# Attention, ReLU² layer and a routed second layer on one core: scatters and stores without order among themselves, another order of second-product quarters, and a later routing step

## The chip, the cores and the metric

One core of a Trainium2 chip runs the whole program. The metric is the device time of one execution in microseconds (us). The engines are TensorE (PE, with its weight loads as PEld), VectorE (DVE), ScalarE (ACT), GpSimd (POOL) and SyncE (SP); DMAs are issued from SP, ACT and POOL. In the listings, POOL issues the indirect DMAs.

## The reference

Three layers follow each other on 4608 tokens of 512 numbers.

```python
scores = scale * np.matmul(q_c, k_c.transpose(0, 1, 2, 4, 3))   # 8 x 8 heads, chunks of 64 rows
attn = softmax(scores); out = np.matmul(attn, v_c)              # becomes x: 4608 x 512
...
h = np.maximum(x @ w_in, 0.0)                                   # 512 -> 2048
x = h * h @ w_out                                               # 2048 -> 512
...
logits = x @ w_gate + modality_bias[modality_id]                # 8 experts
e_idx = np.argmax(logits, axis=1)                               # one expert for each token
for e in range(E):
    mask = e_idx == e
    h = np.maximum(x[mask] @ w1[e], 0.0)                        # 512 -> 1024
    out[mask] = gate_w[mask, None] * (h @ w2[e])                # 1024 -> 512
```

## The kernel before

The 36 tiles of 128 tokens are worked in nine groups of four ("supers" 0 to 8). For a super, PE first makes the first product of the ReLU² layer and then the second. In supers 3 to 8 (`su >= HALVED`) the first product is a scheme of seven products for each of four column groups: 28 steps `prod(su, n, k)` (L621), whose sums DVE and ACT form, whose squares POOL writes to the tile `big` (`square`, L663). Then come 16 steps `mm2(su, t, qq)` (L810) of twelve matmuls each: tile t of the super, quarter qq of the 2048 inner rows. Quarters 0 and 2 read squares of column groups 0 and 1; quarters 1 and 3 read those of groups 2 and 3, which are made last.

The attention of a later super (`s_all`, L457; `xp`, L538, between them softmax work on DVE, ACT and POOL) runs between these steps, and so does the routing of each tile that has its second product: `x2_evac` (read out), `x2_tr` (transpose by DMA), `route_a` (the logits `lp`, L838, and on DVE `lg` and the argmax), `route_b` (the rank of a token in its expert: `rp`, L858 and L859), `route_c` (the row `mt`: token and gate, a COPY on POOL and three small operations on DVE), `route_d` (L884: POOL scatters the 128 rows of `mt` into the table `meta` in DRAM). After 33 tiles the places are looked up: `map_a1`, `map_a1b`, `meta_gather` (POOL), `meta_turn` (a COPY on DVE, L922), `map_a2` (PE transposes into `tp`, L930); then `x_gather`, `x_tr` and `x_sum` fetch, transpose and sum the tokens of a pair of blocks.

In the second layer, work goes in pairs of two blocks of 256 rows of one expert. Pair 0's first products (`first1`) lie between the last `mm2` steps; then `run1` and `run2` (L1199 and L1267) go over 18 more pairs. `pair_o` makes the output rows of a pair on DVE, and `put` (L1293) scatters them to `out`, twice for each pair, on POOL.

What stands after what on an engine is decided at build time: a planner gives each step of PE a planned time T, each other piece of work a due time, and before each PE step it emits what is due (`flush`) and what the step must have (`need`). Engines run their instructions strictly in that order and wait at the first whose semaphores are not there. `rest("a", ...)` is a branch on a value that the data decides (L348: load weights of experts beyond the first, skipped or taken on every engine); its body is skipped in the profiled execution. DMA semaphores are eight in turn for POOL (DMASW0 to 7) and eight for SP and ACT (DMAHW0 to 7): a DMA also waits for the one eight before it on its own kind.

Of the kernel before, what the change touches and what calls it, by code (L numbers as in the profile page):

```python
# [23 lines left out]
HALVED = 3  # L24
# [9 lines left out]
def kernel(  # L34
# [13 lines left out]
    nc = tc.nc  # L48
# [4 lines left out]
    NTILE = NT // 128  # L53
    KD = DM // 128
    KF = DFF // 128
# [6 lines left out]
    SEEN = NTILE - 4  # L62
# [16 lines left out]
    meta = dram.tile([MROWS, 2], F32, name="meta")  # L79
# [321 lines left out]
    done = set()  # L401
# [480 lines left out]
    def route_d(i):  # L882
        a = x2.pop(i)
        nc.gpsimd.indirect_dma_start(  # L884
            out=meta[:, :], out_offset=bass.IndirectOffsetOnAxis(ap=a["di"][:, 0:1].bitcast(U32), axis=0),
            in_=a["mt"], in_offset=None,
        )

    mp = {}
# [17 lines left out]
    def meta_gather(n, name):  # L907
        ri = mp["ri" + name]
        if name == "a":
            mg = pp_b[0][:n]  # L910
        else:
            mg = xtall[:n, 7168:8192].bitcast(F32)
        nc.gpsimd.indirect_dma_start(
            out=mg, out_offset=None, in_=meta.rearrange("(t r) c -> t (r c)", r=PAIR),
            in_offset=bass.IndirectOffsetOnAxis(ap=ri[:n, 0:1].bitcast(U32), axis=0),
        )
        mp["mg" + name] = mg
# [244 lines left out]
    def once(fn, *a):  # L1162
        if a[-1] < PAIRS and (fn, *a) not in gone and a[-1] in pair:
            gone.add((fn, *a))
            fn(*a)

# [124 lines left out]

    def put(t, o):
        nc.gpsimd.indirect_dma_start(  # L1293
            out=out[:, :], out_offset=bass.IndirectOffsetOnAxis(ap=t.bitcast(U32), axis=0),
            in_=o, in_offset=None, bounds_check=NT - 1, oob_is_err=False,
        )

# [259 lines left out]
    for su, (b0, nt, sb) in enumerate(supers):  # L1557
# [12 lines left out]
        for t, qq in M2 if su == 0 else [(t, qq) for t in range(nt) for qq in range(4)]:  # L1570
            steps.append((T, mm2, (su, t, qq)))
            T += STEP
            i = b0 + t
# [11 lines left out]
            d = (4.0, 11.0, 16.0, 19.0, 25.0) if i < NTILE - 2 and i != SEEN - 1 else (4.0, 11.0, 16.0, 19.0, 21.0) if i < NTILE - 1 and i != SEEN - 1 else (4.0, 11.0, 16.0, 19.0, 19.2) if i < NTILE - 1 else (4.0, 8.2, 12.0, 14.0, 14.5)  # L1585
# [39 lines left out]
    with tc.manual_schedule():  # L1625
# [3 lines left out]
        for n, (T, fn, a) in enumerate(steps):  # L1629
# [3 lines left out]
            su = a[0]  # L1633
# [9 lines left out]
            elif fn is first1:  # L1643
                need = [(x2_evac, NTILE - 4), (x2_evac, NTILE - 3)][:1 + (a[0] > 0)]
            elif su >= HALVED:
                need = [(square, su, f, a[1] % 2) for f in range(0, 4 * a[2] + 4, 2)] + [(square, su, KF - 2, 0)] * (a[1] > 0)
# [153 lines left out]
```

## Time and profile before

| what | value |
|---|---|
| median of 3 runs | 1266.74 us (1266.11 to 1266.81) |
| the profiled execution | 1266.4 us, of which the span of the trace is 1264.7 us |
| PE busy | 1173.8 us, 93% of the span; PEld 833.9 us |
| DVE, ACT, POOL busy | 917.6, 706.6, 690.6 us |
| mean granted clock of TensorE | 0.978 |

The span is what the rows below are counted in; the 1.7 us around it belong to the execution's own time. A row of the timeline gives the start, the duration, the engine and line, the operation with its tiles, how many instructions it stands for, and in brackets the idle time of the engine before it with what ended that idle time.

### The profile page before, as it was taken

Reading aid. Unit: us, or ns where it says so; the run is one execution under the profiler, and the core shown is the slowest. Engines: PE = TensorE matmul, PEld = TensorE weight load, DVE = VectorE, ACT = ScalarE, POOL = GpSimd, SP = SyncE. Lnnn points to the kernel's source line nnn. Section 1 sums busy time; section 2 is a strip of 40 time slices with the busy share of each in tenths; the row PEclk is TensorE's granted clock in tenths of the full one; section 3 lists DMA queues with packets and bytes.
Section 4 is the critical chain, followed back from the end, with each engine's and each line's share of the span. In section 5 each row is a group of like instructions: output and inputs, shape, how many; then the busy total and the mean of one; then the engine's idle time right before and its main releaser. Section 6 shows DMA issues by size and latency. Waiting matters only on the chain. (4 is left out here: it accounts for less than half of the span.)

```text
span 1264.7 us, 33052 instructions
## 1 busy us (share of the span) xinstructions
PE 1173.8 (93%) x12910; PEld 833.9 (66%) x12910; DVE 917.6 (73%) x2031; ACT 706.6 (56%) x1392; POOL 690.6 (55%) x641
## 2 busy tenths in 40 slices
PE   5898999999999989899989799999579999999996
PEld 4443444444774754664855664856579999999995
DVE  6899785675696895696886894854577766776663
ACT  6887583574574574574664573633335555555552
POOL 4488374587584484474574483555144455455442
PEclk9899999999899999999999899999799999999998
DMA  9455524324425537436526444255714445733241
GB/s 375 161 161 140 119 53 80 72 51 104 102 44 151 116 80 160 103 82 159 131 70 151 96 72 122 51 186 105 146 44 97 101 93 167 212 93 88 73 102 52
DMA packets 189208, 144.46 MB, mean 114 GB/s; under 512 B 126634, under 2 KB 163534, under 8 KB 187874
## 3 DMA queue, kind: packets, MB, share of 16 engines
q1 hardware_dynamic: 180386, 117.91, 38.8%
q0 software_dynamic: 7632, 20.54, 5.3%
q10 hardware_dynamic: 1008, 3.67, 1.2%
q8 instruction: 103, 1.69, 0.6%
q14 instruction: 79, 0.65, 0.2%
HBM read 204.06 MB, written 34.48 MB: 189 GB/s over the span
## 5 line engine op out<-in xcount | busy, mean ns | idle before, releaser
L810 PEld LDWEIGHTS <-big 128*128 128x128 f16 x1728 | 164.6, 98 | 203.4 <-POOL big L663 9.1
L810 PE MATMUL oo<-big,big 128*128 128x512 f16 x1056 | 237.7, 381 | 3.4 <-POOL big L772 3.4
L1199 PEld LDWEIGHTS <-big 128*128 128x128 f16 x3192 | 192.3, 99 | 20.1 <-issue 16.0
L810 PE MATMUL hh<-big,big 128*128 128x512 f16 x672 | 150.1, 379 | 6.4 <-POOL big L663 6.1
L792 PE MATMUL hh<-xtall,big 128*128 128x512 f16 x576 | 129.3, 382 | 0.1
L1199 PE MATMUL hh<-big,big 128*128 128x128 f16 x2040 | 129.0, 220 | 0.0
L621 PEld LDWEIGHTS <-big 128*128 128x128 f16 x1152 | 112.5, 99 | 22.4 <-issue 7.4
L489 POOL TENSOR_TENSOR ee<-ee,rc 128x512 f32<-128x512 f32 x36 | 39.9, 1108 | 125.1 <-DVE rc L487 71.0
L117 DVE SCALAR_TENSOR_TENSOR stage<-raw,stage 128x256 f16<-128x256 f32 x112 | 73.6, 660 | 41.9 <-ACT stage L114 36.7
L792 PEld LDWEIGHTS <-big 128*128 128x128 f16 x576 | 55.1, 98 | 64.1 <-issue 2.0
L1267 PEld LDWEIGHTS <-xtall 128*128 128x128 f16 x840 | 79.5, 98 | 11.2 <-issue 3.1
L1293 POOL DMA_INDIRECT out_dram<-raw,tib x30 | 35.5, 1183 | 90.7 <-DVE raw L117 79.2
L311 POOL TENSOR_TENSOR raw<-raw 128x256 f32<-128x256 f32 x64 | 52.7, 823 | 55.8 <-DVE stage L117 23.8
L114 ACT ACTIVATE stage<-raw 128x256 f16<-128x256 f32 x112 | 45.3, 410 | 62.3 <-DMA wsp<-stage 35.6
L772 POOL TENSOR_TENSOR big<-sn,big 128x512 f16<-128x512 f32 x48 | 59.4, 1242 | 32.4 <-DVE sn L117 16.1
L1267 PE MATMUL oo<-big,xtall 128*128 128x256 f16 x600 | 73.5, 273 | 2.7 <-DVE raw L117 2.7
L663 POOL TENSOR_TENSOR big<-r,big 128x512 f16<-128x512 f32 x48 | 61.6, 1295 | 26.1 <-ACT big L114 24.1
L663 POOL TENSOR_TENSOR big<-sn,big 128x512 f16<-128x512 f32 x48 | 61.8, 1299 | 24.0 <-ACT big L114 23.9
L114 ACT ACTIVATE big<-hh 128x512 f32<-128x512 f32 x62 | 36.9, 595 | 64.1 <-PE hh L1199 50.9
L1160 POOL TENSOR_TENSOR big<-big 128x512 f16<-128x512 f32 x34 | 39.5, 1181 | 49.6 <-ACT big L114 49.6
L117 DVE SCALAR_TENSOR_TENSOR qkt<-qk,qkt 128x1024 f16<-128x1024 f32 x32 | 47.2, 1475 | 17.3 <-ACT qkt L114 16.8
L884 POOL DMA_INDIRECT meta<-mt,di x36 | 42.2, 1172 | 22.5 <-issue 10.2
(384 smaller groups left out, 2690.3 us busy)
## 6 DMA issues: line engine op xcount, KB each, us to landing
big<-wsp SPq DMA_DIRECT2D x111, 1024.0 KB
big<-wsp SPq DMA_DIRECT2D x37, 512.0 KB
qk<-in_qk_dram SPq DMA_DIRECT2D x34, 512.0 KB
wsp<-stage SPq DMA_DIRECT2D x224, 64.0 KB
x2d<-xs SPq DMA_DIRECT2D x36, 256.0 KB
vv<-in_v_dram SPq DMA_DIRECT2D x34, 256.0 KB
big<-in_w_in_dram SPq DMA_DIRECT2D x16, 512.0 KB
raw<-in_w_out_dram SPq DMA_DIRECT2D x16, 512.0 KB
```

Of the source, the lines that this page charges most:

```text
L114: nc.scalar.activation(out=out, in_=in_, func=func, **kw)
L117: nc.vector.scalar_tensor_tensor(out=out, in0=in0, scalar=s, in1=in1, op0=op0, op1=op1, **kw)
L311: nc.gpsimd.tensor_tensor(out=quad(out_), in0=quad(in0), in1=quad(in1), op=op)
L489: eng.tensor_tensor(out=ee, in0=ee, in1=rc.unsqueeze(2).to_broadcast([128, H, 64]), op=ALU.mult)
L621: nc.tensor.matmul(ps[:, f * 256:f * 256 + 256], lhsT=block(k, la, kk, 2 * n + f), rhs=xa(lb, kk), start=k in (1, 5, 2, 4) and f + m + kk ...
L663: nc.gpsimd.tensor_tensor(out=lo, in0=c, in1=hi, op=ALU.subtract)
L772: nc.gpsimd.tensor_tensor(out=lo, in0=q32.rearrange("p (f n) -> p f n", f=nf), in1=hi, op=ALU.subtract)
L792: nc.tensor.matmul(hp[:, q_ * n:(q_ + 1) * n], lhsT=wi[:, la, kk, f * 128:f * 128 + 128], rhs=x[:, lb, kk, :], start=i == 0, stop=i == 3 * ...
L810: nc.tensor.matmul(ps, lhsT=g[:, la, f, c:c + 128], rhs=wo[:, lb, f, :], start=f == 0 and n == 0, stop=f == KF - 1 and n == 2)
L884: nc.gpsimd.indirect_dma_start(out=meta[:, :], out_offset=bass.IndirectOffsetOnAxis(ap=a["di"][:, 0:1].bitcast(U32), axis=0), in_=a["mt"], ...
L1199: nc.tensor.matmul(ps[:, f * 128:f * 128 + 128], lhsT=WB[0][:, n, la, kk, f * 128:f * 128 + 128], rhs=xa(lb, kk), start=first and f + m + ...
L1267: nc.tensor.matmul(ps, lhsT=hb[:, la, f * 128:f * 128 + 128], rhs=WB[1][:, n, lb, f, :], start=first and f + m == 0, stop=True, skip_group ...
```

## The change

1. The 36 scatters of `route_d` into `meta`, which overlap in no row, are declared free of each other. The gather that reads `meta` is given a dependence on every scatter emitted so far.
2. The stores of `put` into `out` are declared free of each other in the same way.
3. `once` notes what it has emitted, and `first1` needs `x_sum` of pair 0 to stand before it.
4. In supers 3 to 8 the first tile takes its quarters in the order 0, 2, 1, 3 in place of 0, 1, 2, 3.
5. An `mm2` step of these supers needs only the squares of its own quarter to stand before it, not those of all quarters up to it.
6. For all but a few tiles, `route_a` to `route_d` come at 11.5, 18, 21 and 26 us of planned time after the tile's last quarter, in place of 11, 16, 19 and 25.

Since the planner puts all other work around these steps, the order on every engine differs from the third super on.

```diff
@@ route_d
-        nc.gpsimd.indirect_dma_start(
+        ins = nc.gpsimd.indirect_dma_start(
             out=meta[:, :], out_offset=bass.IndirectOffsetOnAxis(ap=a["di"][:, 0:1].bitcast(U32), axis=0),
             in_=a["mt"], in_offset=None,
         )
+        free_of(ins, "meta")
+        scattered.append(ins)
+    scattered = []
@@ meta_gather
+        for x in scattered:
+            tc.add_manual_dep(ins.ins, x.ins.name, mybir.DependencyInfo(mybir.DependencyClass.Sync, mybir.DependencyReason.DATA))
@@ once
             fn(*a)
+            done.add((fn, *a))
@@ put
+    def free_of(ins, group):
+        tc.declare_no_dep(ins.ins, group=group, reason="rows of their own")
+        tc.add_to_no_dep_group(group, ins.ins)
...
+        free_of(ins, "out")
@@ steps
-        for t, qq in M2 if su == 0 else [(t, qq) for t in range(nt) for qq in range(4)]:
+        for t, qq in M2 if su == 0 else [(t, qq) for t in range(nt) for qq in ((0, 2, 1, 3) if su >= HALVED and t == 0 else range(4))]:
...
-            d = (4.0, 11.0, 16.0, 19.0, 25.0) if i < NTILE - 2 and i != SEEN - 1 else ...
+            d = (4.0, 11.5, 18.0, 21.0, 26.0) if i < NTILE - 2 and i != SEEN - 1 else ...
@@ need
-                need = [(x2_evac, NTILE - 4), (x2_evac, NTILE - 3)][:1 + (a[0] > 0)]
+                need = [(x_sum, 0)] + [(x2_evac, NTILE - 4), (x2_evac, NTILE - 3)][:1 + (a[0] > 0)]
             elif su >= HALVED:
-                need = [(square, su, f, a[1] % 2) for f in range(0, 4 * a[2] + 4, 2)] + [(square, su, KF - 2, 0)] * (a[1] > 0)
+                need = [(square, su, f, a[1] % 2) for f in range(4 * a[2], 4 * a[2] + 4, 2)] + [(square, su, KF - 2, 0)] * (a[1] > 0)
```

**Order 1.** POOL in super 5, before. The two DMA rows are scatters of two tiles in a row; `raw` (L311) and `big` (L663) are weight forming and squares, which ACT and PE wait for.

```order
L875 COPY mt<-tok 128x1 x2
L311 TENSOR_TENSOR raw<-raw 128x256 [waits DMAHW3_49,DMAHW1_49,DVE_49]
L489 TENSOR_TENSOR ee_101<-ee_101,rc 128x512 [waits DVE_49,Pool_49]
L884 DMA meta<-mt,di 45312x2 [waits DMASW7_49,Pool_49]
L884 DMA meta<-mt,di 45312x2 [waits DMASW0_49,Pool_49]
L311 TENSOR_TENSOR raw<-raw 128x256 [waits DMAHW1_49,Pool_49]
L311 TENSOR_TENSOR raw<-raw 128x256 [waits DVE_49,Pool_49]
L663 TENSOR_TENSOR big_89<-sn_111,big_89 128x2x256 [waits PE_49,Activation_49]
```

The same stretch of POOL in the changed kernel:

```order
L875 COPY mt<-tok 128x1 [waits DMASW4_49]
L311 TENSOR_TENSOR raw<-raw 128x256 [waits DMAHW5_49,DMAHW1_49,DVE_49]
L884 DMA meta<-mt,di 45312x2 [waits Pool_49]
L311 TENSOR_TENSOR raw<-raw 128x256 [waits DMAHW0_49,Pool_49]
L311 TENSOR_TENSOR raw<-raw 128x256 [waits DVE_49,Pool_49]
L489 TENSOR_TENSOR ee_101<-ee_101,rc 128x512 [waits DVE_49]
```

Each scatter waited for the one before it (DMASW7, DMASW0) and now waits for no DMA; the COPY that refills `mt` waits for the scatter four before, which read that buffer. The next scatter now stands 18 instructions further down.

**Order 2.** PE at the start of super 7, before: behind the last of eight `lp` matmuls of tile 25's `route_a` come `route_b` of the same tile (L858, L859) and 48 `xp` matmuls of attention (L538); eight more `lp` follow before the first `prod` (L621).

```order
L838 MATMUL lp<-wgs,x2t 128x16
L858 LDWEIGHTS ones_h [waits DVE_49]
L858 MATMUL rp<-run,ones_h 128x8 [waits PE_49]
L859 LDWEIGHTS tri_h
L859 MATMUL rp<-oh,tri_h 128x8 [waits DVE_49]
L538 LDWEIGHTS vs_99 [waits Activation_49]
L538 MATMUL xp<-pt_105,vs_99 64x64 [waits DMAHW6_49]
```

The same place in the changed kernel:

```order
L838 MATMUL lp<-wgs,x2t 128x16
L838 LDWEIGHTS x2t
L838 MATMUL lp<-wgs,x2t 128x16
L621 LDWEIGHTS big_87
L621 MATMUL hh_114<-xtall,big_87 128x256
```

The first `prod` now stands right behind the `lp`; the other three pieces come between later `prod` steps. Super 5 begins in the same changed way.

**Order 3.** DVE in super 8 around the branch of `rest("a")`, before: `meta_turn` (L922), the last read-outs of first products (`r`), the two copies of `map_a2`, then the branch.

```order
L922 COPY ee_101<-pp_103 4x256x2 [waits DMASW0_49]
L117 SCALAR_TENSOR_TENSOR r_109<-oo_116,bls,r_109 128x512 [waits PE_49,Activation_49,Pool_49]
L117 SCALAR_TENSOR_TENSOR r_110<-oo_117,bls,r_110 128x512 [waits PE_49,Activation_49,Pool_49]
L117 SCALAR_TENSOR_TENSOR r_110<-r_110 128x512 [waits DVE_49]
L117 SCALAR_TENSOR_TENSOR r_108<-oo_117,bls,r_108 128x512 [waits Pool_49]
L117 SCALAR_TENSOR_TENSOR r_108<-r_108 128x512 [waits DVE_49]
L934 CAST tia<-tp 128x8 [waits PE_49]
L935 COPY fsa<-tp 128x8
L346 TENSOR_LOAD flaga [waits DVE_49]
L348 COMPARE_AND_BRANCH
```

In the changed kernel `meta_turn` is the first instruction behind the branch's body (its lines are five further down):

```order
L348 UNCONDITIONAL_BRANCH
L927 COPY ee_101<-pp_103 4x256x2 [waits DMASW0_49]
L939 CAST tia<-tp 128x8 [waits PE_49]
L940 COPY fsa<-tp 128x8
L1008 TENSOR_TENSOR used<-cum_12022,cum_12025 128x8
```

On PE the four transposes into `tp` stood behind the first `mm2` quarter of super 8 and now stand behind the third.

**Order 4.** POOL at the end of the program, before: the last four stores and the load that follows.

```order
L1293 DMA out_dram<-raw,tib 4608x512 [waits DMASW2_49,DMASW1_49,DVE_49]
L1293 DMA out_dram<-raw,tib 4608x512 [waits DMASW3_49,DMASW2_49,DVE_49]
L1293 DMA out_dram<-raw,tib 4608x512 [waits DMASW3_49,DVE_49]
L1293 DMA out_dram<-raw,tib 4608x512 [waits DMASW4_49,DVE_49]
L1720 TENSOR_LOAD tot [waits DVE_49]
```

And in the changed kernel:

```order
L1303 DMA out_dram<-raw,tib 4608x512 [waits DMASW2_49,DVE_49]
L1303 DMA out_dram<-raw,tib 4608x512 [waits DMASW3_49,DVE_49]
L1303 DMA out_dram<-raw,tib 4608x512 [waits DMASW4_49,DVE_49]
L1303 DMA out_dram<-raw,tib 4608x512 [waits DMASW5_49,DVE_49]
L1731 TENSOR_LOAD tot [waits DVE_49]
```

Before, each store waited for the store ahead of it; now the semaphore that it waits for is the one that it takes over, last used eight DMAs earlier, and DVE.

## Rows read from the trace of the kernel before

**Rows 1.** The page's first part: busy time, share of the span and instructions by engine.

```profile
PE 1173.8 (93%) x12910; PEld 833.9 (66%) x12910; DVE 917.6 (73%) x2031; ACT 706.6 (56%) x1392; POOL 690.6 (55%) x641
```

**Rows 2.** Windows by stage: length, busy PE, PEld, DVE, ACT, POOL, PE clock, DMA.

```profile
416.00:512.00 96.00, 87.56 (x967) 58.31 (x966) 74.80 (x177) 54.78 (x117) 55.27 (x51) 1.00 0.54 121
512.00:605.00 93.00, 88.07 (x947) 58.25 (x946) 74.21 (x169) 53.80 (x114) 55.10 (x52) 0.98 0.48 115
605.00:697.00 92.00, 86.11 (x954) 57.43 (x951) 71.31 (x163) 54.61 (x117) 52.43 (x50) 1.00 0.49 116
697.00:793.00 96.00, 86.91 (x773) 58.01 (x774) 69.46 (x180) 50.38 (x111) 51.68 (x51) 0.96 0.44 95
960.00:1243.00 283.00, 283.00 (x3826) 268.24 (x3825) 199.08 (x345) 153.85 (x289) 141.80 (x122) 1.00 0.45 112
...
531.00:534.40 3.40, 3.40 (x18) 2.43 (x16) 3.26 (x9) 2.38 (x6) 2.65 (x4) 0.50 0.75 167
...
705.30:708.50 3.20, 3.20 (x26) 2.31 (x23) 2.37 (x11) 1.71 (x5) 0.00 (x0) 0.50 0.48 148
```

**Rows 3.** PE's waits: waiting tile <- releaser: us, times, longest.

```profile
PE hh L1199 <- ACT big L114: 12.2, 1, 12.2
...
PE hh L810 <- POOL big L663: 6.1, 4, 2.6
...
PE hh L621 <- DVE sn L117: 1.7, 1, 1.7
```

**Rows 4.** DVE and POOL at the end, timeline: the last operation and the last two stores.

```profile
1255.78 0.88 DVE L117 SCALAR_TENSOR_TENSOR raw<-oo,fsb,ms 128x256 f32<-128x256 f32 x2 [2.12 <-PE oo L1267]
...
1255.04 0.98 POOL L1293 DMA_INDIRECT out_dram<-raw,tib  x1 [2.54 <-DMA out_dram<-raw,tib]
1259.31 0.98 POOL L1293 DMA_INDIRECT out_dram<-raw,tib  x1 [3.29 <-DMA out_dram<-raw,tib]
```

**Rows 5.** The chain that ended last: the store before the last, start and us.

```profile
1255.04 3.50 DMA out_dram<-raw,tib
```

**Rows 6.** POOL in super 5, timeline.

```profile
520.02 1.29 POOL L884 DMA_INDIRECT meta<-mt,di  x1 [0.16 <-POOL ee L489]
524.88 1.35 POOL L884 DMA_INDIRECT meta<-mt,di  x1 [3.57 <-DVE sn L117]
526.25 1.55 POOL L311 TENSOR_TENSOR raw<-raw 128x256 f32<-128x256 f32 x2
```

**Rows 7.** All 36 scatters: from issue to landing.

```profile
DMA to landing us min/median/max: 3.7/4.2/6.7
```

**Rows 8.** ACT and PE behind the two scatters, timeline.

```profile
527.03 0.42 ACT L114 ACTIVATE stage<-raw 128x256 f16<-128x256 f32 x1 [5.14 <-POOL raw L311]
...
529.91 1.73 PE L621 MATMUL oo<-xtall,ee 128*128 128x256 f16 x12 [2.60 <-ACT r L114]
```

**Rows 9.** PE at the start of super 7, timeline.

```profile
701.36 0.18 PE L858 MATMUL rp<-run,ones_h 128*128 128x8 f16 x1 [4.39 <-DVE lg L117]
702.28 0.17 PE L859 MATMUL rp<-oh,tri_h 128*128 128x8 f16 x1 [0.74 <-DVE oh L117]
703.29 0.32 PE L538 MATMUL xp<-pt,vs 64*64 64x64 f16 x4 [0.84 <-ACT vs L114]
704.02 1.38 PE L538 MATMUL xp<-pt,vs 64*64 64x64 f16 x44 [0.41 <-DVE vs L117]
```

**Rows 10.** DVE and PE in super 8 around the branch, timeline.

```profile
829.31 1.60 DVE L922 COPY ee<-pp 4x512 f32<-4x512 f32 x1
...
835.23 0.15 DVE L935 COPY fsa<-tp 128x8 f32<-128x8 f32 x1
841.02 0.17 DVE L1003 TENSOR_TENSOR used<-cum,cum 128x8 f32<-128x8 f32 x1 [5.64 <-issue]
...
833.75 0.41 PE L930 MATMUL tp<-id_f,ee 4*128 4x4 f32 x4
834.09 15.91 PE L810 MATMUL hh<-big,big 128*128 128x512 f16 x72
```

More of the change, by code (lines that the diff above doesn't have):

```diff
@@ L912, in meta_gather @@
             mg = xtall[:n, 7168:8192].bitcast(F32)
-        nc.gpsimd.indirect_dma_start(
+        ins = nc.gpsimd.indirect_dma_start(
             out=mg, out_offset=None, in_=meta.rearrange("(t r) c -> t (r c)", r=PAIR),
@@ L1290, in pair_o @@
             put(t2, o2)
+    def free_of(ins, group):
+        tc.declare_no_dep(ins.ins, group=group, reason="rows of their own")
+        tc.add_to_no_dep_group(group, ins.ins)
     def put(t, o):
-        nc.gpsimd.indirect_dma_start(
+        ins = nc.gpsimd.indirect_dma_start(
             out=out[:, :], out_offset=bass.IndirectOffsetOnAxis(ap=t.bitcast(U32), axis=0),
@@ L1584 @@
                 continue
-            d = (4.0, 11.0, 16.0, 19.0, 25.0) if i < NTILE - 2 and i != SEEN - 1 else (4.0, 11.0, 16.0, 19.0, 21.0) if i < NTILE - 1 and i != SEEN - 1 else (4.0, 11.0, 16.0, 19.0, 19.2) if i < NTILE - 1 else (4.0, 8.2, 12.0, 14.0, 14.5)
+            d = (4.0, 11.5, 18.0, 21.0, 26.0) if i < NTILE - 2 and i != SEEN - 1 else (4.0, 11.0, 16.0, 19.0, 21.0) if i < NTILE - 1 and i != SEEN - 1 else (4.0, 11.0, 16.0, 19.0, 19.2) if i < NTILE - 1 else (4.0, 8.2, 12.0, 14.0, 14.5)
             ch = [(T, x2_evac, (i,)), (T + d[0], x2_tr, (i,)), (T + d[1], route_a, (i,)), (T + d[2], route_b, (i,)), (T + d[3], route_c, (i,)), (T + d[4], route_d, (i,))]
```

## The prediction

> **What bounds the kernel now.** I read the page's engine shares first: PE is busy for 93% of the span, and no other engine for more than 73% [rows 1]. So the time is PE's own work, the time that PE stands still, and the time in which it runs at half speed. The windows by stage say where these are [rows 2]. From 960 to 1243 us, in the pairs of the second layer, PE is busy for all 283 us at full clock: nothing done there for DVE, POOL or the DMAs can shorten anything. In the windows of supers 4, 5, 6 and 7 PE stands still for 8.4, 4.9, 5.9 and 9.1 us (length less busy PE). The clock is 1.00 in supers 4 and 6; in supers 5 and 7 it falls to 0.50 (the lower of the two levels, 1.2 GHz) for some 3.4 us and 3.2 us, each time behind a wait of several us. PE is busy through both stretches, so they cost about half their length, 1.7 and 1.6 us.
>
> Then PE's waits by releaser [rows 3], to see which of them the change can reach. The longest by far, 12.2 us on ACT's `big` in pair 0, hangs on transposes and weight loads that stand in the same order afterwards; I leave it as it is. The squares on POOL (L663) hold up the second products four times, 6.1 us in all. Last I read the end of the program [rows 4, 5]: DVE has made the last output rows at 1256.66 us (1255.78 + 0.88), but the last store begins at 1259.31, held for a landing.
>
> **The change part by part.** *Stores.* The last two stores each waited for the one before [rows 4]: the store of 1255.04 took 3.50 us to land, until 1258.54 [rows 5], and the next began 0.77 us later. Without that wait the last one can begin as far behind DVE's end as it now begins behind the landing, at 1256.66 + 0.77 = 1257.4 instead of 1259.31: **−1.9 us**. Two stores then overlap, from 1257.4 to 1258.5. The slowest landing that I have of an indirect scatter is 6.7 us [rows 7]; should the last store need that in place of 3.5, the 1.9 become +1.3. I take −1.9, since the overlap is only some 1.1 us. The other stores are worth nothing: PE is saturated while they run [rows 2].
>
> *Scatters.* In super 5 two scatters stand back to back (Order 1). The second begins 3.57 us after the first has been issued [rows 6]; the row names DVE as releaser, but 520.02 plus a median landing of 4.2 [rows 7] is 524.2, and what the instruction waits for is the first one's landing. Behind it POOL's weight-forming rows are late, ACT stands idle for 5.14 us for them and then reads out a first product, and PE waits 2.60 us for that [rows 8]; the half-speed stretch from 531.0 follows [rows 2]. Gap and clock, 2.60 + 1.7 = 4.3 us, should go: the second scatter is 18 instructions away and waits for no landing. The new wait of the `mt` copy on the scatter four before costs nothing: 36 scatters spread over some 750 us against a slowest landing of 6.7 [rows 7]. The gather's new dependences name scatters that the old chain had it wait for anyway.
>
> *Later routing, with the order that it draws after it.* At the start of super 7, `route_b` of tile 25, an attention step and `route_a` of tile 26 all stood before the first `prod` (Order 2), and PE waited 4.39 + 0.74 + 0.84 + 0.41 = 6.4 us for DVE and ACT to work through them [rows 9]; with 1.6 us of half clock that is 8.0. Now `prod` comes first, with its inputs long there, and those pieces fall between products, where PE has work while DVE computes. Super 5 opened with a smaller bundle of the same kind, worth about 1.6 us of its 4.9. Taken straight from the rows, supers 5 and 7 give 4.3 + 1.6 + 8.0 = 13.9 us. But a reshuffled order makes waits of its own. The nearest row for that is super 6, which already opened with `prod` and still stands still for 5.9 us [rows 2]. Were supers 4, 5 and 7 to become like it, they would give (8.4 − 5.9) + (4.9 + 1.7 − 5.9) + (9.1 + 1.6 − 5.9) = 2.5 + 0.7 + 4.8 = 8.0. The bounds are 8.0 and 13.9; I take **−10**, nearer to the homogeneous supers, because what is moved must be done somewhere on the same DVE and ACT. Its DMAs (the transposes of `x2_tr`) keep their planned time.
>
> *Quarter order and the relaxed need.* Tile 0's quarter 1, which waited for POOL's last squares, now comes third, but quarter 3 is still last and needs the last square of all. PE only reaches it as soon as before, and waits for the same POOL row. I take **0**; all 6.1 us [rows 3] is the bound if POOL gets through earlier, and a loss of 2 us if one more scatter falls before the last square (1.3 us each [rows 6]).
>
> *Super 8 and its branch.* Here the change adds a wait. In the kernel before, `meta_turn` ran on DVE at 829.31, the transposes of `tp` on PE at 833.75 without a wait, and the branch came behind: DVE stood for 5.64 us, from 835.38 to 841.02 [rows 10]. Now `meta_turn` stands behind the branch, and PE's transposes behind the third quarter (Order 3). DVE reaches the branch earlier by the copy and the two small ones (1.60 + 0.3), at about 833.5; it is through at 839.1, and the copy ends at 840.7. PE, which had three quarters and the transposes done by about 839.4, waits for it with all remaining `mm2` queued behind: some 1.7 us later than before. The 1.7 us that PE waited in super 8 for DVE's `sn` [rows 3], behind the look-up that is now later, may go and make DVE as much earlier (then 0); a fall of the clock would add another 1.7, and a later `x_sum` up to 1. Bounds 0 and +4.4; I take **+1.7**.
>
> This is where the Trainium skill speaks otherwise. The row shows 5.64 us of idle DVE at the branch [rows 10]. The page Advanced Engine Details and Errata, in Control Flow Timing, puts a compare-and-branch at about 0.1 us; an estimate by that page would have DVE through by 833.7, no wait on PE, and a sum lower by 1.7 us. The trace disagrees with it here, at least for a branch over a long body, and I go by the trace.
>
> Sum: −1.9 − 10 + 0 + 1.7 = −10.2 on the profiled execution's 1266.4, so 1256.2; its time stands 0.3 below the median of 1266.74, which makes the forecast 1256.5.
>
> **The rivals.** *A, the forecast:* 1256.5, own range 1251 to 1261.
>
> *B, the reshuffle gives back.* Supers 4 to 7 get waits of their own as large as those removed, and only waits that are taken away by themselves stay gone: stores 1.9 and scatters 4.3, less 1.7 in super 8: 1266.7 − 4.5 = 1262. For it: super 6 lost 5.9 us without any bundle. Against it: super 7's 6.4 us lie in one place, on a chain that PE had no work to cover.
>
> *C, slower.* `x_gather`, `x_tr` and `x_sum` of pair 0 come later, since the look-up does, and `first1` now has `x_sum(0)` ahead of it in the order. If the transposes of pair 0 collide with the weight loads as those of a later pair do, which is what lies behind the 12.2 us wait in pair 0 [rows 3], PE waits as long once more, and the clock would fall: 1256.5 + 12.2 + 3.4 = 1272. It decides as soon as the loss exceeds the 10.2 us won. Against it: in the order they move by some 4 us, and a sum that ends 4 us later delays the first of `first1` by at most about 1.
>
> *D, the squares too.* With quarter 1 out of the way and POOL no longer stopped at scatters, the 6.1 us go: 1256.5 − 6.1 = 1250.
>
> *E, no change.* PE is 93% busy, the planner moves its waits about, and what super 7 gives is lost in supers 3 to 6 and 8: within 0.2% of 1266.7.
>
> **How the numbers follow.** A 0.50, B 0.16, C 0.12, D 0.11, E 0.11. A measurement of this kernel can tell about 0.2% (2.5 us) from no change. Faster by more: A, B and D, 0.77; within it: E, 0.11; slower: C, 0.12. The predicted time is A's, 1256.5. The range from 1248 (D, with the supers at their bound of 13.9 in part) to 1265 leaves out C and a part of E, under 2 in 10; A's own range is given above.
>
> **What would show it.** Right: the last store begins within a us of DVE's last output; POOL's scatters never idle for a landing; no wait over 2 us at the start of super 7, and the clock at 1.00 in the windows of supers 5 and 7; idle PE of 5 to 6 us in each of supers 4 to 7; `tp` on PE released by DVE's copy, 1 to 3 us late. Wrong: idle sums of supers 4 to 7 that are unchanged (B or E), a wait of PE for `x_sum` or for the transposes near the start of `first1` (C), or no more waits on L663 (D). What would upset it most is a long wait in a new place, by a product whose transposed inputs are formed later than before, and the half clock behind it.

## The result: 1.0% slower

The changed kernel takes 1275.43 us (median of 12 runs, 1269.53 to 1281.85) against 1262.62 us of the kernel before (12 runs beside it, 1256.3 to 1266.81). The ratio is 1.0102, with an interval of 1.0079 to 1.0125. The forecast was 1256.5 us, faster.

The traces below are of one execution each, and executions of one kernel spread by some 10 us (the two ranges above). The ratios rest on medians; a difference of 2 or 3 us between the same window of two traces says little by itself.

The profiled execution spans 1275.2 us, 10.5 more than the 1264.7 of before. To place these 10.5 us I cut both spans where the same work begins: at the first product of supers 4, 5, 6, 7 and 8, at the first product of `first1`, and at the end of that pair's last long wait. These are the windows of the kernel before (length, busy PE, PEld, DVE, ACT, POOL, PE clock, DMA share, GB/s):

```profile
416.07:511.86 95.79, 87.35 (x966) 58.13 (x965) 74.80 (x177) 54.64 (x117) 55.27 (x51) 1.00 0.54 121
511.86:604.74 92.88, 87.95 (x950) 58.15 (x947) 73.95 (x170) 53.94 (x114) 55.10 (x52) 0.98 0.48 114
604.74:705.57 100.83, 88.58 (x1013) 59.44 (x1012) 76.62 (x184) 57.76 (x124) 53.15 (x51) 0.98 0.49 116
705.57:792.04 86.47, 83.73 (x713) 55.36 (x710) 63.75 (x155) 46.55 (x101) 50.32 (x49) 0.98 0.44 94
792.04:855.62 63.58, 61.88 (x479) 44.22 (x478) 42.34 (x132) 29.75 (x56) 35.29 (x34) 1.00 0.41 122
855.62:902.00 46.38, 34.20 (x383) 24.15 (x380) 17.91 (x70) 13.82 (x31) 16.71 (x19) 0.90 0.76 139
902.00:1264.70 362.70, 343.33 (x4536) 323.43 (x4534) 247.83 (x472) 183.16 (x347) 169.92 (x147) 0.98 0.40 101
```

And these are the same windows of the changed kernel:

```profile
418.19:513.54 95.35, 88.90 (x956) 58.45 (x955) 73.88 (x167) 54.62 (x115) 54.74 (x51) 0.96 0.45 114
513.54:603.36 89.82, 86.19 (x960) 57.41 (x957) 70.78 (x171) 53.39 (x115) 52.51 (x51) 1.00 0.46 119
603.36:701.44 98.08, 88.83 (x961) 58.87 (x958) 77.24 (x175) 55.45 (x117) 55.98 (x54) 0.95 0.50 116
701.44:795.93 94.49, 85.80 (x768) 56.72 (x765) 66.20 (x171) 50.67 (x112) 51.70 (x50) 0.96 0.42 96
795.93:867.82 71.89, 63.72 (x482) 45.27 (x480) 44.95 (x139) 32.23 (x62) 35.33 (x36) 0.95 0.37 108
867.82:914.00 46.18, 34.20 (x378) 24.15 (x378) 19.55 (x68) 11.99 (x28) 15.62 (x18) 0.89 0.72 139
914.00:1275.20 361.20, 343.16 (x4536) 323.01 (x4534) 248.49 (x472) 184.99 (x347) 170.18 (x147) 0.98 0.41 101
```

Line by line the differences are −0.4, −3.1, −2.8, +8.0, +8.3, −0.2 and −1.5 us; the windows begin 2.1 us later. Super 5 is shorter and its clock is back at 1.00, as forecast. The bundle ahead of super 7's products lay at the end of the third window of before, and its matmuls now lie in the fourth: PE's instructions fall from 1013 to 961 in the third and rise from 713 to 768 in the fourth. So supers 6 and 7 are read together: 187.3 us before, 192.6 after, +5.3. By the forecast they should have been some 8 us shorter without the bundle's waits. Super 8 is longer by 8.3 us. PE's idle time in supers 4 to 7 (length less busy PE) is 28.4 us in sum before and 28.0 after: the waits have moved, not gone. The half clock has moved too: before it fell in supers 5 to 7, now it falls in 4, 6, 7 and 8.

PE's waits of the changed kernel, to be read against [rows 3] (waiting tile, releaser: us in total, times, longest):

```profile
PE hh L621 <- ACT sn L114: 15.6, 5, 7.4
PE hh L1205 <- ACT big L114: 12.0, 1, 12.0
PE hh L810 <- POOL big L663: 10.3, 4, 5.1
...
PE tp L935 <- DVE ee L927: 5.1, 1, 5.1
```

The last of these is new, the first has a longest wait of 7.4 us, and the squares on POOL hold PE up for 10.3 us in place of 6.1, 5.1 of them at once in super 4, with the half clock behind. The 12 us in pair 0 stayed.

**Where supers 6 and 7 lose.** The timeline of the changed kernel around the fourth product of super 6, all engines (start, us, engine, line, operation, idle time ahead of it and its releaser):

```profile
601.39 1.04 POOL L884 DMA_INDIRECT meta<-mt,di  x1 [0.15 <-POOL raw L311]
602.68 2.70 SPq L378 DMA_DIRECT2D wsp<-stage  x4
608.82 0.42 ACT L114 ACTIVATE stage<-raw 128x256 f16<-128x256 f32 x1 [6.70 <-DMA wsp<-stage]
...
613.84 0.41 ACT L114 ACTIVATE stage<-raw 128x256 f16<-128x256 f32 x1
614.15 0.68 ACT L114 ACTIVATE sn<-hh,bls 128x512 f32<-128x512 f32 x1
614.88 2.72 PE L621 MATMUL hh<-xtall,vs 128*128 128x256 f16 x12 [7.43 <-ACT sn L114]
```

Read it from below. PE waits 7.43 us for the read-out `sn<-hh` of the first product, which frees the bank that the fourth needs. That read-out is a late step of a queue on ACT whose head is a weight-forming step, `stage<-raw` at 608.82. The head stood for 6.70 us until one of the stores `wsp<-stage` had landed and its buffer was free; nine activations, from 608.82 to 613.84, then go through ahead of the read-out. Two of the nine form weights (`stage`); the others belong to attention and to the read-out of second products. The four stores were issued from 602.68 on, 1.3 us behind a scatter of routing rows. The same place in the kernel before:

```profile
602.22 0.42 ACT L114 ACTIVATE stage<-raw 128x256 f16<-128x256 f32 x1 [1.60 <-DMA wsp<-stage]
608.96 0.41 ACT L114 ACTIVATE stage<-raw 128x256 f16<-128x256 f32 x1
609.26 1.26 ACT L114 ACTIVATE sn<-hh,bls 128x512 f32<-128x512 f32 x2
609.99 1.47 PE L621 MATMUL hh<-xtall,vs 128*128 128x256 f16 x12 [0.23 <-issue]
```

There ACT waits for a store once, ahead of super 6's first product (604.74); then come steps of attention and one `stage` step that waits for nothing, and PE waits 0.23 us. A scatter was issued there too, at 603.35, and a store of 603.99 released its waiter, DVE, only 6.6 us later; but it was not the one that ACT had at its head. So at super 6 the scatter and the late store are in both kernels, and the order on ACT is what differs. At super 7 the same happens: ACT idle for 6.54 us until 704.64, behind a store of 698.73 with a scatter at 698.95, read-out at 710.25, PE held for 5.45 us.

The clock falls behind each of these waits (windows of the changed kernel, 4 us each, behind the waits of supers 6, 7 and 8):

```profile
612.00:616.00 4.00, 1.12 (x6) 0.81 (x6) 2.96 (x10) 3.50 (x9) 0.00 (x0) 0.50 0.06 18
616.00:620.00 4.00, 4.00 (x21) 2.81 (x20) 3.69 (x7) 0.99 (x2) 1.04 (x1) 0.50 0.67 225
...
711.00:715.00 4.00, 4.00 (x27) 2.89 (x27) 3.04 (x9) 2.02 (x4) 0.00 (x0) 0.50 0.25 78
...
848.00:852.00 4.00, 3.49 (x12) 1.55 (x13) 2.46 (x14) 0.00 (x0) 3.29 (x3) 0.50 0.37 115
```

In the first two PE is busy for 1.12 + 4.00 = 5.1 us at 0.50, the lower of the two levels (1.2 GHz), and so loses at least half of that, 2.6 us; in the other two at least 2.0 and 1.7 us. The waits and what follows them cost 7.43 + 2.6, 5.45 + 2.0 and, in super 8, 5.06 + 1.7, some 24 us. Gone are the bundle's 6.4 + 1.6 [rows 9, 2], super 5's 2.60 + 1.7 [rows 8, 2] and 2.4 us at the last store, some 15. The difference, some 9.5, is near the 10.5 us between the spans; other, smaller waits moved as well, so this is an account and no proof.

**Super 8.** The branch on DVE, the copy behind it and PE's transposes in the changed kernel, which answer to [rows 10]:

```profile
841.09 0.87 DVE L117 SCALAR_TENSOR_TENSOR r<-r 128x512 f32<-128x512 f32 x1
847.58 0.87 DVE L927 COPY ee<-pp 4x512 f32<-4x512 f32 x1 [5.62 <-issue]
848.51 0.59 PE L935 MATMUL tp<-id_f,ee 4*128 4x4 f32 x4 [5.06 <-DVE ee L927]
```

DVE stands at the branch for 5.62 us, from 841.96 on, and PE waits for the copy behind it. It is not the branch instruction that takes this time. The branches on DVE, by their line in the changed kernel (engine, operation, times: shortest, median and longest in ns, first and last start):

```profile
L348 DVEq COMPARE_BRANCH  x4: 47/53/66, 841.7 to 947.5; - x4
```

Each takes 0.047 to 0.066 us, and in the kernel before the same. The idle time lies behind the second one. The trace doesn't name what ends it. A DMA queue for instructions brings three packets of 8 KB in that time, beside other transfers at some 417 GB/s; whether DVE waits for these packets no run shows.

**The end.** DVE's last operation and the last store of the changed kernel, which answer to [rows 4]:

```profile
1267.05 0.88 DVE L117 SCALAR_TENSOR_TENSOR raw<-oo,fsb,ms 128x256 f32<-128x256 f32 x2 [2.12 <-PE oo L1273]
1268.20 0.99 POOL L1303 DMA_INDIRECT out_dram<-raw,tib  x1 [2.01 <-DVE raw L117]
```

DVE ends at 1267.93 and the last store begins 0.27 us later, not 2.65 as before.

### The profile page after: what moved, and what is told of

Read it like the earlier page. It is cut to its first block, busy times and chain, and to the rows that moved or that the text cites. A ratio compares the mean times of both kernels' runs of the same rounds, so it can differ in the third digit from the quotient of the medians.

```text
span 1275.2 us, 33050 instructions
## 1 busy us (share of the span) xinstructions
PE 1178.2 (92%) x12910; PEld 833.7 (65%) x12910; DVE 927.0 (73%) x2031; ACT 706.5 (55%) x1392; POOL 691.5 (54%) x641
## 5 line engine op out<-in xcount | busy, mean ns | idle before, releaser
L810 PEld LDWEIGHTS <-big 128*128 128x128 f16 x1728 | 165.8, 99 | 209.0 <-POOL big L663 12.2
L810 PE MATMUL hh<-big,big 128*128 128x512 f16 x672 | 154.1, 388 | 10.3 <-POOL big L663 10.3
L621 PEld LDWEIGHTS <-big 128*128 128x128 f16 x1152 | 112.1, 99 | 18.9 <-issue 3.9
L1273 PEld LDWEIGHTS <-xtall 128*128 128x128 f16 x840 | 79.7, 98 | 11.3 <-issue 3.1
L663 POOL TENSOR_TENSOR big<-sn,big 128x512 f16<-128x512 f32 x48 | 60.5, 1272 | 39.2 <-ACT big L114 35.9
L311 POOL TENSOR_TENSOR raw<-raw 128x256 f32<-128x256 f32 x64 | 54.4, 849 | 49.4 <-DVE stage L117 35.1
L663 POOL TENSOR_TENSOR big<-r,big 128x512 f16<-128x512 f32 x48 | 62.1, 1305 | 16.5 <-ACT big L114 14.7
L117 DVE SCALAR_TENSOR_TENSOR qkt<-qk,qkt 128x1024 f16<-128x1024 f32 x32 | 55.8, 1744 | 10.9 <-ACT qkt L114 10.5
L114 ACT ACTIVATE ee<-ee 128x512 f32<-128x512 f32 x46 | 28.7, 624 | 45.0 <-DVE ee L470 43.4
```

The lines of the kernel that those rows point to most:

```text
L114: nc.scalar.activation(out=out, in_=in_, func=func, **kw)
L117: nc.vector.scalar_tensor_tensor(out=out, in0=in0, scalar=s, in1=in1, op0=op0, op1=op1, **kw)
L311: nc.gpsimd.tensor_tensor(out=quad(out_), in0=quad(in0), in1=quad(in1), op=op)
L621: nc.tensor.matmul(ps[:, f * 256:f * 256 + 256], lhsT=block(k, la, kk, 2 * n + f), rhs=xa(lb, kk), start=k in (1, 5, 2, 4) and f + m + kk ...
L663: nc.gpsimd.tensor_tensor(out=lo, in0=c, in1=hi, op=ALU.subtract)
L810: nc.tensor.matmul(ps, lhsT=g[:, la, f, c:c + 128], rhs=wo[:, lb, f, :], start=f == 0 and n == 0, stop=f == KF - 1 and n == 2)
```

## The experiments

The ratios are to the kernel before, run beside each. `after` in a diff's first line means that it is made on the changed kernel; the others are made on the kernel before.

**The parts alone.** e1_stores has the free stores alone, and e2_scatters the free scatters with the gather's dependences (one scatter 1.5 planned us later).

```diff
 put()      # e1_stores
+        free_of(ins, "out")
 route_d()  # e2_scatters
+        free_of(ins, "meta")
+        scattered.append(ins)
```

> The kernel before with the stores of put free of each other and nothing else. Theory R (the later routing's new order on the engines makes the whole loss, the freed DMAs cost nothing): the last store begins about 1.9 us earlier, the time falls by 1 to 2.5 us (ratio 0.998 to 0.999). Rival F (freed DMAs collide and land later, and that makes the loss): no gain or slower by some us.

> The kernel before with the scatters of route_d free of each other; the second of the two adjacent ones in super 5 stands two POOL instructions later, PE's order is the old one. Theory R: PE's wait of 2.6 us in super 5 and the half clock behind it go, 3 to 4.3 us less. Rival F: scatters that overlap land later and POOL or the stores behind them lose what is won; the same time or slower.

e1_stores: 1260.6 us, ratio 0.9986 (0.997 to 1.0002), some 1.8 us of 1263; the size fits the term of 1.9, but the interval reaches no change. e2_scatters: 1255.23 us, 0.9944 (0.992 to 0.9967), some 7 us: the scatters alone make the kernel faster, and the waits of [rows 8] are gone from its trace. Its super 5 is hardly shorter for that, 92.5 us against 92.9, with other waits (1.23 and 1.53 us) and a half clock of its own; in e8_free_all below super 5 takes 89.8 us.

e3_delay has the later delays alone, e4_quarters the order of quarters with the relaxed need of squares. e3_delay leaves out the need that ties the first expert's products in pair 0 to `x_sum(0)`, since it belongs to the change: they may take rows that are not summed yet, and its stretch from `first1` on is not comparable. e4_quarters leaves that need out as well, other than its expectation says.

```diff
# e3_delay
-            d = (4.0, 11.0, 16.0, 19.0, 25.0) if i < NTILE - 2 and i != SEEN - 1 else ...
+            d = (4.0, 11.5, 18.0, 21.0, 26.0) if i < NTILE - 2 and i != SEEN - 1 else ...
# e4_quarters
-[(t, qq) for t in range(nt) for qq in range(4)]
+[(t, qq) for t in range(nt) for qq in ((0, 2, 1, 3) if su >= HALVED and t == 0 else range(4))]
-for f in range(0, 4 * a[2] + 4, 2)]
+for f in range(4 * a[2], 4 * a[2] + 4, 2)]
```

> The kernel before with the later routing (11.5, 18, 21, 26) and nothing else: scatters and stores still wait for each other, quarters in the old order. Theory R: this alone makes the new order, so super 8 is some 8 us longer, the first products of supers 6 and 7 some 9 us, and the whole 11 to 15 us slower than before (ratio about 1.010). Rival Q (the quarters' order costs, by the waits on squares in supers 4 and 7, 4 to 6 us): only 5 to 8 us slower. Rival F: near the time of before.

> The kernel before with x_sum of pair 0 ahead of first1, the quarter order 0, 2, 1, 3 and the relaxed need, and nothing else. Theory R: within 2 us of before, since quarter 3 still waits for the last square. Rival Q: 4 to 6 us slower by waits on squares. A gain of 3 to 6 us would say that quarter 1 stood in the way after all.

e3_delay: 1272.38 us, 1.0084 (1.0054 to 1.0115); its trace has the waits of the changed kernel, 7.90 us in super 6, 5.54 in super 7 and 4.65 for `tp`. At the first product of `first1`, ahead of the stretch that is not comparable, it is at 866.0 us, 10.4 later than the kernel before; the changed kernel is 12.2 later. So the delays alone make most of the loss. e4_quarters: 1264.05 us, 1.0014 (0.9994 to 1.0034), no gain and no measurable loss.

**The two waits by their inputs.** e5_branch emits the look-up with the branch 0.9 planned us later, so that the copy again stands ahead of it. e6_scatter issues each scatter 6 planned us later, and e7_both does both.

```diff
# after: e5_branch, e7_both
-            at_time(TM1 + 2.0, rest, "a", ...
+            at_time(TM1 + 2.9, rest, "a", ...
# after: e6_scatter, e7_both
-            d = (4.0, 11.5, 18.0, 21.0, 26.0) if ...
+            d = (4.0, 11.5, 18.0, 21.0, 32.0) if ...
```

> The changed kernel with the branch of rest(a) due 0.9 us of planned time later, so that meta_turn stands ahead of it on DVE again and two squares ahead of it on ACT and POOL; PE's work keeps its order. Theory B (the branch ahead of meta_turn makes the loss of super 8): PE's wait of 5.1 us for the copy and the half clock behind it go, 6 to 8 us less than the changed kernel, ratio to the kernel before about 1.004 in place of 1.010. Rival: the small operations of the look-up on DVE are late by themselves, and the transposes still wait 3 us or more; 0 to 3 us less.

> The changed kernel with route_d at 32 in place of 26: the scatters come 6 us of planned time later, other engines keep their order but for a few rows. Theory S (at the starts of supers 6 and 7 a scatter makes the weight stores beside it land late, ACT waits for those ahead of its read-outs, and PE for the read-outs): the waits of 7.4 and 5.5 us there and the half clock go, 9 to 15 us less than the changed kernel, ratio about 1.000. Rival O (ACT's order alone does it: weight forming ahead of the read-out waits for some landing in any case): the waits stay over 3 us, 0 to 5 us less.

> The changed kernel with the branch later (as in the run on the branch) and the scatters later (as in the run on the scatters). If theories B and S both hold, the two gains add: 15 to 22 us less than the changed kernel, ratio about 0.993 to 0.998. If either falls, the sum is short by that part.

e5_branch: 1278.97 us, 1.0111 (1.0089 to 1.0134). The wait for `tp` is gone, as theory B had it, and super 8 takes 64.6 us in place of 71.9, but the window of `first1` grows from 46.2 to 54.4: the gain is given back there, and the foreseen 1.004 is missed. e6_scatter: 1280.85 us, 1.0116 (1.0074 to 1.0159). No gain overall, where theory S foresaw about 1.000: the wait of super 7 becomes 7.47 us, behind a store issued 1.0 us after a scatter, and super 3 grows from 88.5 to 93.0 us. But at super 6, where the last scatter ahead of the four stores is 32 us away, the rows are these (e6_scatter, timeline):

```profile
607.52 1.87 SPq L378 DMA_DIRECT2D wsp<-stage  x4
609.49 0.42 ACT L114 ACTIVATE stage<-raw 128x256 f16<-128x256 f32 x1 [2.37 <-DMA wsp<-stage]
615.93 2.72 PE L621 MATMUL hh<-xtall,vs 128*128 128x256 f16 x12 [3.45 <-ACT sn L114]
```

From the first of the four stores to ACT's release it takes 2.0 us here, and took 608.82 − 602.68 = 6.1 us beside the scatter; PE waits 3.45 in place of 7.43 us. So 3.45 us stay with the order on ACT, and the late store makes the rest. e7_both: 1278.08 us, 1.0107 (1.008 to 1.0135), with 2.68 and 2.96 us at the two starts, and the last wait of `first1` still at 11.3; of the foreseen 0.993 to 0.998 nothing came.

**Without the reordering.** e8_free_all is the kernel before with free scatters and free stores (one scatter 1.5 planned us later, as in e2_scatters).

```diff
+        free_of(ins, "meta")
+        scattered.append(ins)
...
+        free_of(ins, "out")
```

> The kernel before with stores and scatters free of each other (the second of the two adjacent scatters two POOL instructions later), and its order on PE kept. If the two gains measured apart add: 1.8 + 7 = 9 us less than before, ratio about 0.993. If a store's landing and a scatter's have nothing to do with each other it can't be less than the scatters alone, 0.9944.

1256.76 us, 0.9944 (0.9924 to 0.9964): faster than both kernels. The interval holds 0.993 and 0.9944, so whether the two gains add is open.

**Order or scatters.** By then two theories were left for the waits at the starts of supers: the order on ACT (O), and the scatters that delay the weight stores (S); and one for the drain at the first expert (G). e9_forming_away keeps weight forming out of ACT's queue ahead of each later super and leaves the scatter of tile 20 in the old chain, e10_gather_first moves one scatter behind two gathers, e11_scatter_step moves the scatters back by one planned us and leaves the order of PE, DVE and SP as it is.

```diff
# after: e9_forming_away
-        free_of(ins, "meta")
+        if i != 20:
+            free_of(ins, "meta")
-                if "regs" not in mp or ...
+                if any(s - 8.0 < t < s + 1.0 for s, _ in span[HALVED + 1:]) or "regs" not in mp or ...
# after, with the edit of e5_branch: e10_gather_first
-(T + d[4], route_d, (i,))]
+(T + d[4] + (6.0 if i == 32 else 0.0), route_d, (i,))]
# after: e11_scatter_step
-            d = (4.0, 11.5, 18.0, 21.0, 26.0) if ...
+            d = (4.0, 11.5, 18.0, 21.0, 25.0) if ...
```

> The changed kernel, with the gated product of the formed second-projection weights (the part events, by which ScalarE copies, transposes' inputs and stores are made ready) kept out of the 8 planned us before each later super's first product (one scatter, that of row tile 20, left in its old chain). Theory O (the changed kernel loses at the starts of supers 6 and 7 because its order puts ten such ScalarE steps ahead of the read-out that the fourth product waits for): the waits of 7.43 and 5.45 us for ScalarE at the fourth product of supers 6 and 7 fall to under 2 each, and the span falls by about 9 us against the changed kernel, to near 1266, ratio to before about 1.003. Theory S (the same ten steps would be through in time if the weight stores beside a scatter did not land late): the order matters little, waits of 3 to 6 us stay at some starts of supers, span 1270 to 1276, ratio about 1.009.

> The kernel of e5_branch with one scatter, that of row tile 32, issued behind the first two row gathers of the early expert instead of just ahead of them; every other engine keeps its order. Theory G (in e5_branch the gathers issued 1.3 us behind that scatter landed in 5.2 to 5.8 us, so that the transposes after them fell behind the first expert's weight loads and the drain at the first expert grew by 8 us): the gathers land in 3.5 to 4 us, the drain falls back to 44 to 47 us, span near 1267, ratio to before about 1.005. Rival (the drain is bound by the bytes of seven weight loads that start no earlier, whatever the gathers do): the drain stays at 52 to 55 us and the ratio at 1.011.

> The changed kernel with the scatters alone put back to the older planned delay (25.0 instead of 26.0), the three other routing steps later as in the change; TensorE, VectorE and SyncE keep the changed kernel's order, only GpSimd's differs, and nine lines of ScalarE's. Theory O: the same gaps of 7.4 and 5.5 us at the fourth products of supers 6 and 7, ratio 1.010. Theory S: the gaps change by 3 us or more each, in either direction, since other weight stores now fall beside a scatter; the sum of the two between 4 and 14 us.

e9_forming_away: 1262.25 us, 0.9976 (0.9949 to 1.0002), by the two ratios some 1.3% below the changed kernel. ACT at the start of super 6 in its trace:

```profile
609.19 0.68 ACT L114 ACTIVATE sn<-hh,bls 128x512 f32<-128x512 f32 x1
...
615.89 0.42 ACT L114 ACTIVATE stage<-raw 128x256 f16<-128x256 f32 x1 [2.41 <-DMA wsp<-stage]
```

The read-out is at 609.19, no weight store is awaited ahead of it, and no wait of PE at the starts of supers 6 and 7 is over 2.17 us. So theory O holds for the two waits. (Its ten weight-forming steps are nine activations of which two form weights; moving those moved others too.) The time is better than it foresaw, and only in part for its reason. Against the trace of the changed kernel super 6 is 0.3 us shorter, since its wait for squares rose to 4.04 us; super 7 is 4.9 us shorter, super 8, where the wait for `tp` falls to 1.70 us, 4.7, and what follows 3.8, while the supers ahead take 2.7 us more. e11_scatter_step: 1275.63 us, 1.0082 (1.0055 to 1.011), with 8.37 and 4.91 us at the two starts, as theory O had it. It says less of S than was hoped, for at super 6 the scatter kept its place between the same two rows of POOL and just ahead of the same four stores. With the old delay for the scatters the loss stays, so it comes with the other three delays. e6_scatter and e9_forming_away together say that the 7.43 us take both: a weight-forming step at the head of ACT's queue, and a store that lands late beside a scatter.

e10_gather_first: 1269.99 us, 1.0017 (1.0 to 1.0034), against 1.0111 of e5_branch. First the rows of e5_branch, then those of e10_gather_first (scatter, first gather, the early expert's transposes on SP, its weight loads on ACT's queue, and the end of ACT's last wait):

```profile
876.01 1.03 POOL L884 DMA_INDIRECT meta<-mt,di  x1 [0.96 <-POOL mt L875]
877.35 0.98 POOL L1123 DMA_INDIRECT big<-x2d,tia  x1 [0.31 <-PE oo L810]
882.15 0.91 ACTq L1091 DMA_DIRECT2D big<-wsp  x2
883.29 6.29 SPq L1131 DMA_TRANSPOSE big<-big  x2
913.34 0.60 ACT L114 ACTIVATE big<-hh 128x512 f32<-128x512 f32 x1 [18.73 <-DMA big<-big]
```

```profile
882.72 0.99 POOL L1123 DMA_INDIRECT big<-x2d,tia  x1 [2.24 <-PE oo L810]
885.26 1.00 POOL L884 DMA_INDIRECT meta<-mt,di  x1 [0.30 <-issue]
887.91 2.92 SPq L1131 DMA_TRANSPOSE big<-big  x2
889.18 0.91 ACTq L1091 DMA_DIRECT2D big<-wsp  x2
905.29 0.60 ACT L114 ACTIVATE big<-hh 128x512 f32<-128x512 f32 x1 [5.24 <-DMA big<-big]
```

With the scatter ahead of the gathers the first transpose is issued 1.1 us behind the first weight load, the two take 6.29 us to issue, and ACT waits 18.73 us for them; with it behind, the first transpose goes 1.3 us ahead of the loads and the wait is 5.24 us. Moving this one scatter is worth 0.9%, and the drain is shorter as theory G foresaw. Its reason is shown in part only: from the first gather to the first transpose it is 5.94 us and then 5.19, not 3.5 to 4, while the first load comes 4.80 us and then 6.46 us behind that gather, so most of the shift is loads that come later. Nor does the order of transposes and loads by itself set the wait. In e6_scatter, the changed kernel and e4_quarters the first transpose goes 0.2 us ahead of the loads in each, and PE's last wait of `first1` is 6.8, 12.0 and 15.4 us. What sets this wait is open.

**Combinations.** e12_free_away puts the edit of e9_forming_away on e8_free_all. e13_no_delay is the whole change with the delays of before (one scatter 1.5 planned us later). e14_away_branch has the edits of e9_forming_away and e5_branch, e15_all_three that of e10_gather_first as well (in both the scatter of tile 20 keeps its old chain).

> The kernel of e8_free_all (older delays and older quarter order, scatters and stores free), with the forming of the second-projection weights kept out of the 8 planned us before each later super's first product as in e9_forming_away. Theory O: the starts of supers 6, 7 and 8 lose under 2 us each, about 1249, ratio 0.989. Theory S: no gain over e8_free_all, 0.994, since what is moved away comes back beside other scatters. The drain at the first expert may take any gain ahead of it back.

> The whole change without the later routing delays: free scatters and stores, other quarter order, relaxed and added needs, delays as before (the scatter of row tile 17 1.5 planned us later). Its order on every engine is that of e8_free_all but for the quarters of first tiles. If the delays are the only edit that costs time: ratio 0.994 as e8_free_all, within 0.003. Rival (quarters and needs cost together with free scatters what they did not cost alone in e4_quarters): above 0.998.

> e9_forming_away with the branch emitted later as in e5_branch (behind the copy of the gathered rows). If the three places add up: super 8 shorter by 2 to 4 us than in e9_forming_away, but one scatter now stands just ahead of the first gathers of the early expert, so that the drain takes some of it back: ratio 0.995 to 1.000. If the drain takes all of it: 0.998 or above, with the last wait at the first expert near 8 to 12 us.

> e14_away_branch with the scatter of row tile 32 issued behind the first gather of the early expert. If the scatter ahead of the gathers is what lengthens the drain: the last wait at the first expert falls to 4 to 6 us and the ratio to 0.990 to 0.994, below e8_free_all. Rival: no change against e14_away_branch, since the gather behind the two scatters then is the late one.

e13_no_delay: 1261.12 us, 0.9938 (0.991 to 0.9966), the ratio of e8_free_all. Everything in the change but the delays is worth −0.6%, and the delays on top of it +1.6%. e14_away_branch: 1264.47 us, 0.9953 (0.9921 to 0.9985), and e15_all_three: 1264.03 us, 0.9967 (0.9943 to 0.9991): with the places mended the new order too is faster than the kernel before, though no better than e8_free_all. Super 8 of e14_away_branch, foreseen 2 to 4 us shorter than in e9_forming_away, is longer, 69.6 against 67.2 us. The last wait of `first1` is 9.38 us in the one and 6.75 in the other, in the foreseen direction, but the times do not differ: the rival named for e15_all_three stands as to the time. e12_free_away: 1269.49 us, 1.0041 (1.0012 to 1.007), which theory O did not foresee. No wait of a product at a super's start is over 2.4 us, yet super 5 takes 100.1 us in place of the 89.8 of e8_free_all (supers 6 and 7 together are equal, 186.5 and 186.3 us). There PE waits 2.36 and 2.32 us for read-outs by ACT, at 521.35 and 531.64, with the half clock behind each: two waits of the same kind, 12 and 22 us into the super, where e8_free_all has none over 1.3 us. So keeping the same work away from the starts helps the new order and hurts the old one; how the moved steps made the two waits was not followed.

## Why the prediction was wrong

**Stores, −1.9.** Right in mechanism: the last store follows DVE by 0.27 us. e1_stores measures 1.8 us, within an interval that reaches zero.

**Scatters, −4.3 of the −10.** The wait of 2.60 us is gone, as forecast, and e2_scatters gives 0.9944, some 7 us. Those 7 us are no proof of the term, though: super 5, where it was to be won, is 0.4 us shorter in that trace and 3.1 us in that of e8_free_all, and where the rest is won was not followed.

**Later routing, the rest of the −10: the step that failed.** The prediction took the waits of the bundle ahead of super 7's products out (they did go) and bounded what the new order would cost by super 6 of the kernel before, "the nearest row", so that its bounds were all gains, 8.0 to 13.9. It looked at the order of POOL, PE and DVE and never at ACT's. There the new order puts weight-forming steps, which wait for DMA landings, ahead of the read-outs. Super 6, the model for the others, itself got a wait of 7.43 us. Supers 4 to 7, forecast at −10, measure −0.4 − 3.1 − 2.8 + 8.0 = +1.7 us. Their idle sum is unchanged (28.4 and 28.0 us), which the prediction had named as a sign of B or E: as to these supers rival B, that the reshuffle makes waits as large as those it removes, describes what happened, though not the time (1262). The delays measure +0.84% alone (e3_delay) and +1.6% on top of the rest (e13_no_delay against the whole change). Why they cost more in company is open: the two kernels differ in the last wait of `first1` (7.34 us in e3_delay, 12.0 in the changed kernel), but e3_delay is not comparable there.

The last sentence of the prediction had named this as what would upset it most, "a long wait in a new place ... and the half clock behind it", but gave it no price; rival C, which carried the slower side, was another mechanism, and did not occur: pair 0's wait for its transposes stayed at 12 us.

**Super 8, +1.7: the right mechanism, mis-sized.** Super 8 is longer by 8.3 us. The idle of DVE at the branch, taken from the trace as 5.64 us, was 5.62, so the forecast was right to count it. It was wrong to set it against the 0.1 us that the Trainium skill gives for a compare-and-branch (Advanced Engine Details and Errata, Control Flow Timing). The trace has these instructions at 0.047 to 0.066 us, which does not contradict the page; the 5.6 us are idle time behind them, and they are not the same at every passage: 3.26 us in e9_forming_away and 3.72 in e14_away_branch. PE reached its transposes when it was forecast to: 843.45 − 795.93 = 47.5 us into super 8, against 839.4 − 792.04 = 47.4. What was wrong is when DVE gets to the branch: 41.5 us into the super by the forecast, 841.96 − 795.93 = 46.0 in the trace. The forecast took 1.9 us of work away from before and nothing else; but DVE was busy for 38.7 of these 46.0 us, against 38.2 of 43.3 before, so other work had come ahead of the branch, and 2.3 us more of idle time. So PE waits 5.06 us, and the clock falls. That the 7.3 us which e5_branch takes out of super 8 come back in the `first1` window was not in the prediction at all; that stretch ends with transposes on SP beside weight loads on ACT's queue, and its last wait on PE lies between 4 and 18 us in these kernels, for reasons that stay open.

**Quarters, 0.** Right for the edit alone (e4_quarters; e13_no_delay is at the ratio of e8_free_all). The wait for squares rose from 6.1 to 10.3 us in the changed kernel, which is beyond the bound of +2; with the old order and free scatters it is 5.1 and with the delays alone (e3_delay) 10.1, so the rise goes with the order of the delays.

## What to carry to other kernels

When a delay in a planner moves, read the new order on every engine that waits for a DMA, not only on the two that the bottleneck waits for: an in-order queue with a landing at its head holds up all that stands behind it. Price a reordering with bounds of both signs, since it takes known waits away and cannot show the new ones. A gain ahead of a stretch that waits for DMAs can be given back there (7.3 us out of super 8, 8.2 us more in `first1`), so measure that stretch with it.

## What the runs showed of the hardware

Stores issued beside a small scatter land late. At super 6 four 64 KB stores released ACT 6.1 us after the first had been issued behind a scatter, and 2.0 us after it where no scatter was near (e6_scatter). Over the whole trace of the kernel before, 20 weight stores were waited for. From issue to release the four with a scatter issued at most 5 us ahead took 3.1 to 6.6 us, one with a scatter 6 us ahead 4.8, and the fifteen with none within 8 us 1.5 to 4.0. In sum ACT waits for weight stores as follows, in the kernel before and then in the changed one (waiting engine and tile: us, times):

```profile
  ACT stage L114: 35.6, 17
```

```profile
  ACT stage L114: 48.9, 15
```

The 13 us more go with waits that are no more in number, but longer. What in the DMA system makes the stores late was not tested.
